# Gate/up units of an FFN: product order 1, 2, 5, 6, 7, 3, 4 instead of 1, 5, 6, 2, 7, 3, 4, gate half before up half, and a new order of VectorE's work

## The chip, the cores and the metric

The kernel runs on one NeuronCore of a Trainium2 chip. Its engines work side by side, each through its own queue in program order: TensorE (matmuls, PE in the profile, with the weight loads as PEld), VectorE (DVE), ScalarE (ACT), GpSimd (POOL) and SyncE (SP), which issues nearly all DMAs. They wait for each other by semaphores. The metric is the device time of one execution in microseconds (us); the time before is the median of three runs.

## The reference

A transformer block with adaptive layer norm: six modulation rows from a small product, a linear-attention block, and a gated FFN. All inputs are bfloat16; the sequence has S = 2048 rows, D = 1024, F = 3584.

```python
mod = (_silu(c) @ w_mod).reshape(c.shape[0], 6, 1, -1)      # sa, ca, ga, sb, cb, gb
h = _layernorm(x) * (1 + ca) + sa
x = x + ga * _A_ref(h, A_wqkv, A_wo)                        # linear attention, 32 heads
h = _layernorm(x) * (1 + cb) + sb
x = x + gb * _B_ref(h, B_w_gate, B_w_up, B_w_down)

def _B_ref(x, w_gate, w_up, w_down):
    return _gelu(x @ w_gate) * (x @ w_up) @ w_down
```

## The kernel before

The program is written as one list of operations with the memory ranges that they read and write; every operation waits for the earlier ones it depends on. Each engine runs its own operations in the order of the list. Only the attention part (up to the mark at L1679) is put into another order by a planner with costs and due times (`reorder`, L1862); the FFN stages, which the change touches, run exactly as written.

**Gate/up stage** (about 242 to 605 us of the span). It has 28 units: 2 halves of the sequence (1024 rows each) by 14 blocks of 256 columns of F. A unit computes gate and up for 256 columns and 1024 rows by a Winograd form of the 2x2 block product, with 7 products instead of 8, each for gate (t = 0) and up (t = 1). A product is 4 matmuls of 128x128 weights by 512 columns per t, so a unit has 56 matmuls (`prod`, L1464). Products 1 and 2 are plain bfloat16 ones. Products 5, 6, 7, 3, 4 are of sums and differences and run in float32r: `t_sum` (L1438, two 512-wide VectorE ops for each of the differences 0, 1, 2, 4; number 3 is a plain copy on ScalarE, L1427) makes the five weight operands `tp0` to `tp4` for products 5, 6, 7, 3, 4, and `s_sum` (L1418, 8 ops of 1024 wide per half of the sequence) makes the four state operands. `ar_copy` (L1404) is ScalarE's copy of the fifth.

PSUM's eight banks are four pairs, gate and up each: BA for products 1 and 2, BE for product 5, BB for products 6, 7 and 4, BC for product 3. What joins them:

- `pcp` (L1470, ScalarE) copies product 1 from BA to BB, and product 2 then adds onto BA, product 6 onto BB.
- `escp` (L1473, ScalarE) evicts product 5 to SBUF.
- `padd` (L1476, VectorE): after product 6, BC = BB + product 5; after product 7, BE = BB + product 5. Product 3 adds onto BC, product 4 onto BB.
- `gelu` (L1481, ScalarE) of the gate bank and `y_out` (L1485, VectorE), the product with the up bank, for four outputs: BA after product 2, BE after 7, BC after 3, BB after 4. The last output's `y_out` is held back and emitted in the next unit, behind the first half of its product 1; `y_store` then sends the unit's result to HBM.

A matmul that writes a bank, as the first of its product, waits until the bank has been read: product 2 for `pcp`, product 7 for `padd` after product 6, product 4 for `padd` after product 7, and `pcp(1)` itself waits for the held `y_out` that reads the up bank of BB. Product 6 needs both copies of `pcp`.

`unit(v)` (L1502) walks the products in `order`; behind each product it emits what belongs to it and then runs hooks, small pieces of other work spread over the units with `hook(v, k, fn)` (run behind product k of unit v). ScalarE's layer norm for the second half of the sequence lies in units 1 to 8 (sum behind product 6, square sum behind 7, normalisation behind 3, the last followed by a DMA transpose on SP); the modulation `mod2` in units 5 to 9; the second half's `s_sum` in units 10 to 13; from unit 14 on the weight sums of the down stage (`b_sum`, L1577, one 512-wide op per hook, four per block of the down weights) and their raw loads (`raw_load`, L1560 to 1567, SP). Unit 0 has its own order (ORD0: 1, 2, 5, 6, then 7, 3, 4 with the last attention chunks between) and is left alone by the change of the default order.

**Down stage** (from about 605 us): the same Winograd form with 8 row blocks; `dprod` (L1611), `dpcp` (L1644), `descp` (L1648), `dpadd` (L1652), `a_sum` (L1605) play the parts of `prod`, `pcp`, `escp`, `padd`, `s_sum`; `lws(n)` emits the next n of the remaining weight sums.

Of the kernel before, what the change touches and what calls it, by code (L numbers as in the profile page):

```python
# [346 lines left out]
def bass_adaLN_cond__linear_attn_block__geglu_ffn__prompt_kernel(  # L347
# [18 lines left out]
    with ExitStack() as es:  # L366
# [410 lines left out]
        def mod2(p, h, c0, n, dc0=0, dc1=NDC):  # L777
            mods(h2ap, r_h2p, (p, h), sc2, c0 * P, (c0 + n) * P, dc0, dc1, "h2")
# [320 lines left out]
        late = {}  # L1099
# [298 lines left out]
        ND2 = NDC // 2  # L1398
        S32 = [[t_.ap().bitcast(f32) for t_ in r_] for r_ in SS]
        T32 = [t_.ap().bitcast(f32) for t_ in TP]  # L1400

        def ar_copy(p):
            for k in (0, 2):
                sch.op(A, lambda e, k=k: e.activation(A22R[p][:, k:k + 2, :], H2[p][1][:, ND2 + k:ND2 + k + 2, :], ACTF.Copy),  # L1404
                       rd=r_h2(p, 1, ND2 + k, ND2 + k + 2), wr=r_ar(p, k, k + 2), note=f"arcp {p}.{k}")

# [38 lines left out]
        def prod(u, t, k, dcs=range(ND2)):  # L1445
            p = u // NFP
            if k in (1, 2):
                r = k - 1
                lhs = lambda dc: (WT[u % 2][:, t, r * ND2 + dc, 0:P], r_wt(u % 2, t, t + 1, r * ND2 + dc, r * ND2 + dc + 1))
                rhs = lambda dc: (H2[p][0][:, r * ND2 + dc, :], r_h2(p, 0, r * ND2 + dc, r * ND2 + dc + 1))  # L1450
            else:
                ti = {5: 0, 6: 1, 7: 2, 3: 3, 4: 4}[k]
                lhs = lambda dc: (TP[ti][:, t, dc, :], r_tp(ti, t, t + 1))
                if k == 4:
                    rhs = lambda dc: (A22R[p][:, dc, :], r_ar(p, dc, dc + 1))
                else:
                    si = {5: 0, 6: 1, 7: 2, 3: 3}[k]
                    rhs = lambda dc: (SS[p][si][:, dc, :], r_ss(p, si, dc, dc + 1))
            b = {1: BA, 2: BA, 5: BE, 6: BB, 7: BB, 4: BB, 3: BC}[k] + t
            fresh = k in (1, 5)  # L1460
            o = None
            for dc in dcs:
                (l_, rl), (r_, rr) = lhs(dc), rhs(dc)
                o = sch.op(T, lambda e, l_=l_, r_=r_, dc=dc: e.matmul(PS(b), l_, r_, start=fresh and dc == 0, stop=dc == ND2 - 1, skip_group_check=True),  # L1464
                           rd=rl + rr, pwr=(pr(b) if dc == 0 else ()), note=f"ffn u{u} P{k} {t} dc{dc}", overwrite_ok=True)
            if dcs[-1] == ND2 - 1:
                pset_writer(b, o)
# [31 lines left out]
        def hook(v, k, fn):  # L1499
            HK.setdefault((v, k), []).append(fn)  # L1500

        def unit(v, order=(1, 5, 6, 2, 7, 3, 4)):  # L1502
            more = v + 1 < 2 * NFP
            for k in order:
                if isinstance(k, tuple):
                    wo_chunk(*k)
                    continue
                if callable(k):
                    k()
                    continue  # L1510
                late = v == 0 and k == 2
                gb_, gk, yl, yh = (None, 1, 0, 0) if late else {2: (BA, 0, 0, 0), 7: (BE, 1, 1, 1), 3: (BC, 0, 1, 0), 4: (BB, 0, 0, 1)}.get(k, (None, 1, 0, 0))
                if k > 2:
                    for dc in range(ND2):
                        for t in range(2):
                            prod(v, t, k, [dc])
                for t in range(2):
                    if k < 3:
                        prod(v, t, k)
                    if k == 1:  # L1520
                        if held[0]:
                            held[0]()
# [12 lines left out]
                if k == 2 and v + 2 < 2 * NFP:  # L1535
                    wt_dma(v + 2)
                if k == 4:
                    held[0] = lambda: y_out(ig, BB, v, 0, 1)
                elif gb_ is not None:
                    y_out(ig, gb_, v, yl, yh)  # L1540
                if k == 1:
                    if v == 0:
                        ar_copy(0)
                    else:
                        t_sum(v, 4)
                if more:
                    if k == (3 if v == 0 else 5):
                        t_sum(v + 1, 0)
                    if k == (3 if v == 0 else 2):
                        t_sum(v + 1, 1)  # L1550
                    if k == 3:
                        t_sum(v + 1, 3)
                        t_sum(v + 1, 2)
                for f_ in HK.pop((v, k), ()):
                    f_()

# [156 lines left out]
        for i in range(4):  # L1713
            hook(i + 1, 2, lambda i=i: x1_store(i))
        for n in range(4):
            hook(5 + n // 2, (7, 4)[n % 2], lambda n=n: mod2(1, 0, 0, 4, 2 * n, 2 * n + 2))
        hook(9, 7, lambda: mod2(1, 1, 0, 4, 0, 3))
        hook(9, 4, lambda: mod2(1, 1, 0, 4, 3, 5))
        hook(9, 6, lambda: mod2_act(1, 1, 0, 4, 5, 6))
        hook(9, 3, lambda: mod2_act(1, 1, 0, 4, 6, 8))  # L1720
        hook(10, 3, lambda: ar_copy(1))
        for n in range(8):
            i, j = divmod(n, 2)
            hook(10 + n // 2, (7, 4)[n % 2], lambda i=i, j=j: s_sum(1, i, j))
        hook(12, 2, lambda: raw_load(0))
        hook(13, 2, lambda: raw_load(1))
        ew = b_sums(range(NEA + 2))
        for n in range(4 * NEA):
            v, k = 14 + n // 2, (7, 4)[n % 2]
            hook(v, k, lambda: next(ew)())  # L1730
            if n % 4 == 3 and 2 + n // 4 < NEA:
                hook(v, k, lambda n=n: raw_load(2 + n // 4))
# [3 lines left out]
        hook(24, 2, lambda: raw_load(6))  # L1736
        hook(26, 2, lambda: raw_load(7))
        hook(26, 7, lambda: next(ew)())
        hook(26, 4, lambda: next(ew)())
        V_ = 2 * NFP - 1  # L1740
        hook(V_, 5, lambda: a_sum(0, 0, NEA))
        hook(V_, 5, lambda: next(ew)())
        hook(V_, 6, lambda: (raw_load(8), a_sum(1, 0, NEA), a_sum(4, 0, NEA)))
        hook(V_, 2, lambda: (raw_load(9), raw_load(10), next(ew)(), next(ew)()))
        hook(V_, 7, lambda: (raw_load(11), raw_load(12)))
        hook(V_, 3, lambda: (next(ew)(), next(ew)()))
        hook(V_, 4, lambda: next(ew)())

        for v in range(2 * NFP):
# [20 lines left out]
        dprod(0, 5, 0, NEA)  # L1770
        descp(0)
        a_sum(2, 0, NEA)
        lws(3)
        dprod(0, 6, 0, NEA)
        dpadd(0, BC)
        a_sum(3, 0, NEA)
        dprod(0, 2, 0, NEA)
        for l in range(2):
            y_load(1, l, 0, NEA)
# [1 line left out]
        dpadd(0, BE)  # L1781
        dprod(0, 3, 0, NEA)
        dprod(0, 4, 0, NEA)
        lws(6)
        for k in range(NEA, NKP):
            for s_ in range(2):
                for c in range(2):
# [148 lines left out]
```

## Time and profile before

| | |
|---|---|
| median of the runs (lowest to highest) | 791.15 us (790.52 to 792.69) |
| profiled execution, its own time | 790.65 us |
| its span, first to last instruction | 788.8 us |
| TensorE busy | 775.3 us (98%) |
| VectorE, ScalarE, GpSimd busy | 636.1 (81%), 342.5 (43%), 43.9 us (6%) |
| granted TensorE clock | 1.000 |
| gate/up unit in steady state (units 14 to 26) | 12.60 us |

Busy times are sums over the span; matmuls are pipelined, so a row's length (0.38 to 0.39 us for a 512-wide matmul) is longer than the step from one matmul to the next. In a group of n like matmuls the step is the group's length less one row, over n - 1. A timeline line reads: start in us, length in us, engine, source line, operation, output <- inputs, shape, how many were merged, and in square brackets how long the engine sat idle before it and what ended that wait. A waits line reads: engine and line, what it waited for, the total in us, how often, the longest. In the chain of work each piece is a stretch in which the end of the program hung on the named engine.

### The profile page before, as it was taken

The numbers are of one execution on the slowest core, as the hardware profiler recorded it, in microseconds if no ns is written. First come the engines' busy times: TensorE is split into PE (matmuls) and PEld (weight loads), VectorE is DVE, ScalarE is ACT, GpSimd is POOL, SyncE is SP. The second block draws the span as 40 slices with busy tenths as digits, with TensorE's granted clock in tenths as the row PEclk, the third lists the DMA queues.
The fourth block names the chain that finished last, engine by engine and source line by source line (L and its number), as shares of the span: only waits on it lengthen the run. The fifth ranks groups of instructions, "written<-read, shape, count | busy, mean of one in ns | idle before, by whom it ended". The sixth has DMA issues, their size and how long they took to land. (4 is left out here: it accounts for less than half of the span.)

```text
span 788.8 us, 11024 instructions
## 1 busy us (share of the span) xinstructions
PE 775.3 (98%) x3840; PEld 495.6 (63%) x3904; DVE 636.1 (81%) x1078; ACT 342.5 (43%) x582; POOL 43.9 (6%) x126
## 2 busy tenths in 40 slices
PE   7999999999999999999999999999999999999998
PEld 4444445666445667777666767777776576666766
DVE  6799899983598877888999888898989786567664
ACT  2497743232583576675634444453545011111110
POOL 2131300000230001010000000000000000000000
PEclk9999999999999999999999999999999999999999
DMA  9789749836596378556355557555546354434340
GB/s 288 246 175 240 169 109 237 207 72 130 133 256 167 116 205 253 154 135 170 99 151 148 159 168 233 141 147 147 142 117 203 102 170 128 140 113 139 109 141 27
DMA packets 211407, 125.93 MB, mean 160 GB/s; under 512 B 70668, under 2 KB 201748, under 8 KB 211352
## 3 DMA queue, kind: packets, MB, share of 16 engines
q1 hardware_dynamic: 211336, 125.23, 58.5%
q8 instruction: 31, 0.51, 0.3%
q14 instruction: 24, 0.20, 0.1%
q10 hardware_dynamic: 16, 0.00, 0.0%
HBM read 88.35 MB, written 23.22 MB: 141 GB/s over the span
## 5 line engine op out<-in xcount | busy, mean ns | idle before, releaser
L1464 PE MATMUL ps_all<-ss,tp 128*128 128x512 f32 x896 | 226.2, 403 | 1.1 <-ACT ps_all L1470 0.6
L1464 PEld LDWEIGHTS ps_all<-ss,tp 128*128 128x128 f32 x896 | 167.7, 188 | 43.6 <-ACT ps_all L1470 2.2
L1481 ACT ACTIVATE ge<-ps_all 128x512 f32<-128x512 f32 x112 | 66.7, 596 | 134.7 <-DVE ps_all L1476 83.2
L1611 PE MATMUL ps_all<-bt,xs 128*128 128x512 f32 (+1 forms) x485 | 118.5, 399 | 0.9 <-DVE ps_all L1652 0.9
L1611 PEld LDWEIGHTS ps_all<-bt,xs 128*128 128x128 f32 x485 | 91.1, 188 | 22.3 <-DVE ps_all L1652 1.4
L1485 DVE TENSOR_TENSOR yr<-ge,ps_all 128x512 bf16<-128x512 f32 x112 | 76.7, 685 | 31.6 <-PE ps_all L1464 17.8
L1476 DVE TENSOR_TENSOR ps_all<-ps_all,es 128x512 f32<-128x512 f32 x112 | 72.4, 691 | 8.7 <-PE ps_all L1464 7.5
L1438 DVE TENSOR_TENSOR tp<-wt 128x512 fp32r<-128x512 bf16 x112 | 72.1, 684 | 1.3
L1438 DVE TENSOR_TENSOR tp<-wt,tp 128x512 fp32r<-128x512 bf16 x112 | 72.0, 683 | 0.0
L1611 PE MATMUL ps_all<-bx,yl 128*128 128x512 bf16 (+2 forms) x269 | 59.8, 360 | 0.7
L965 PE MATMUL ps_all<-h1T,wq 128*128 128x512 bf16 x256 | 56.7, 379 | 0.0
L914 PE MATMUL ps_all<-wk,h1T 128*128 128x512 bf16 x239 | 55.3, 379 | 1.1 <-DMA wk<-in_A_wqkv_dram 0.5
L1299 PE MATMUL ps_all<-w,pq 128*128 128x512 bf16 x251 | 55.9, 379 | 0.4
L1644 ACT ACTIVATE ps_all<-ps_all 128x512 f32<-128x512 f32 x8 | 4.7, 582 | 117.4 <-PE ps_all L1611 117.4
L1464 PE MATMUL ps_all<-ar,tp 128*128 128x512 f32 x224 | 55.3, 389 | 0.0
L903 ACT ACTIVATE eb<-ps_all 128x512 f32<-128x512 f32 x64 | 36.4, 593 | 37.1 <-PE ps_all L914 15.4
L1464 PE MATMUL ps_all<-h21a,wt 128*128 128x512 bf16 x210 | 50.1, 380 | 1.0
L1464 PE MATMUL ps_all<-h20a,wt 128*128 128x512 bf16 x210 | 50.0, 380 | 0.9
L1464 PEld LDWEIGHTS ps_all<-ar,tp 128*128 128x128 f32 x224 | 42.1, 188 | 8.7
L1470 ACT ACTIVATE ps_all<-ps_all 128x512 f32<-128x512 f32 x56 | 32.6, 582 | 30.6 <-DVE yr L1485 15.4
L965 PEld LDWEIGHTS ps_all<-h1T,wq 128*128 128x128 bf16 x256 | 25.0, 98 | 30.0
L1299 PEld LDWEIGHTS ps_all<-w,pq 128*128 128x128 bf16 x256 | 24.7, 98 | 30.3 <-issue 0.5
(146 smaller groups left out, 903.8 us busy)
## 6 DMA issues: line engine op xcount, KB each, us to landing
wt<-in_B_w_gate_dram SPq DMA_DIRECT2D x28, 512.0 KB, 4.0
wt<-in_B_w_up_dram SPq DMA_DIRECT2D x28, 512.0 KB, 5.2
scr_y<-yr SPq DMA_DIRECT2D x56, 256.0 KB, 2.9
yl<-scr_y SPq DMA_DIRECT2D x12, 832.0 KB, 4.3
wmst<-in_w_mod_dram SPq DMA_DIRECT2D x6, 1024.0 KB, 5.7
wmq<-in_w_mod_dram SPq DMA_DIRECT2D x8, 512.0 KB, 6.1
rb<-scr_rd SPq DMA_DIRECT2D x32, 128.0 KB, 2.9
scr_x<-xall SPq DMA_DIRECT2D x4, 1024.0 KB, 7.1
```

The source lines that it names most:

```text
L903: sch.op(A, lambda e: e.activation(EB[i][:, :], PS(bank), ACTF.Exp), prd=pr(bank), wr=rng, note=f"{note}.exp")
L914: o = sch.op(T, lambda e, dc=dc: e.matmul(PS(bank), H1[sg][:, ci, dc, :], W_[:, dc, jg * 512:(jg + 1) * 512], start=(dc == 0), stop=(dc == ...
L965: o = sch.op(T, lambda e, dc=dc: e.matmul(PS(b), WQ[:, dc, qc * P:(qc + 1) * P], H1[sg][:, :, dc, :], start=(dc == 0), stop=(dc == NDC - 1 ...
L1299: last[half] = sch.op(T, lambda e, g=g, half=half: e.matmul(PS(b0 + half), PQ[sg][:, g, ci * P:(ci + 1) * P], W2[:, g, half * 512:(half + ...
L1438: sch.op(V, lambda e, t=t: e.tensor_tensor(TP[k][:, t, :, :], in0[:, t, :, :], in1[:, t, :, :], ALU.subtract), rd=r0[t:t + 1] + (r1[t:t + ...
L1464: o = sch.op(T, lambda e, l_=l_, r_=r_, dc=dc: e.matmul(PS(b), l_, r_, start=fresh and dc == 0, stop=dc == ND2 - 1, skip_group_check=True) ...
L1470: sch.op(A, lambda e: e.activation(PS(BB + t), PS(BA + t), ACTF.Copy), prd=pr(BA + t), pwr=pr(BB + t), note="pcp")
L1476: sch.op(V, lambda e: e.tensor_tensor(PS(dst + t), PS(BB + t), ES[t][:, :], ALU.add), prd=pr(BB + t), rd=r_2k(OFF_ES[t], f"es{t}"), pwr=pr ...
L1481: sch.op(A, lambda e: e.activation(GE[i][:, :], PS(b), ACTF.Gelu_apprx_tanh), prd=pr(b), wr=r_2k(OFF_GE[i], f"ge{i}"), note="gelu")
L1485: sch.op(V, lambda e: e.tensor_tensor(YR[:, 2 * (v % 2) + l, h * SGW:(h + 1) * SGW], GE[i][:, :], PS(b + 1), ALU.mult), rd=r_2k(OFF_GE[i], ...
L1611: pend_ = sch.op(T, lambda e, l_=l_, r_=r_, i=i: e.matmul(PS(b, c0, c1), l_, r_, start=fresh and i == 0, stop=i == n - 1, skip_group_check ...
L1644: sch.op(A, lambda e: e.activation(PS(BB + t), PS(BA + t), ACTF.Copy), prd=pr(BA + t), pwr=pr(BB + t), note="pcp")
```

## The change

- **Order of products** of units 1 to 27: 1, 2, 5, 6, 7, 3, 4 instead of 1, 5, 6, 2, 7, 3, 4.
- **Gate before up.** Products 5, 6, 7, 3, 4 ran matmul by matmul alternately for gate and up; now all four gate matmuls come first, as products 1 and 2 already had it. The GELU of product 7's output is emitted behind the gate half.
- **VectorE's weight differences.** Difference 0 for the next unit moves from behind product 5 to behind product 7. Differences 1 and 2 move from the unit before (behind products 2 and 3) into the unit that uses them: behind product 1, after the held last output of the unit before, and ahead of difference 4.
- **Hooks.** Those behind product 4 move to behind product 2 of the next unit (modulation, state sums, weight sums with their raw loads). `ar_copy(1)` is split over units 10 and 11, behind product 6. In unit 27 the raw loads and weight sums are spread over products 2, 6, 7, 3 and 4 in another way.
- **Down stage.** Of the nine weight sums that `lws` emits ahead of the plain products, three stood ahead of the first `dpadd`; now one follows behind `a_sum(3)`, and eight behind product 4.

```diff
-        def unit(v, order=(1, 5, 6, 2, 7, 3, 4)):
+        def unit(v, order=(1, 2, 5, 6, 7, 3, 4)):
...
-                gb_, gk, yl, yh = (None, 1, 0, 0) if late else {2: (BA, 0, 0, 0), 7: (BE, 1, 1, 1), 3: (BC, 0, 1, 0), 4: (BB, 0, 0, 1)}.get(k, (None, 1, 0, 0))
-                if k > 2:
-                    for dc in range(ND2):
-                        for t in range(2):
-                            prod(v, t, k, [dc])
+                gb_, gk, yl, yh = (None, 1, 0, 0) if late else {2: (BA, 0, 0, 0), 7: (BE, 0, 1, 1), 3: (BC, 0, 1, 0), 4: (BB, 0, 0, 1)}.get(k, (None, 1, 0, 0))
                 for t in range(2):
-                    if k < 3:
-                        prod(v, t, k)
+                    prod(v, t, k)
...
                     else:
+                        t_sum(v, 1)
+                        t_sum(v, 2)
                         t_sum(v, 4)
                 if more:
-                    if k == (3 if v == 0 else 5):
+                    if k == (3 if v == 0 else 7):
                         t_sum(v + 1, 0)
-                    if k == (3 if v == 0 else 2):
-                        t_sum(v + 1, 1)
                     if k == 3:
                         t_sum(v + 1, 3)
-                        t_sum(v + 1, 2)
...
         for n in range(4):
-            hook(5 + n // 2, (7, 4)[n % 2], lambda n=n: mod2(1, 0, 0, 4, 2 * n, 2 * n + 2))
+            hook(5 + (n + 1) // 2, (7, 2)[n % 2], lambda n=n: mod2(1, 0, 0, 4, 2 * n, 2 * n + 2))
         hook(9, 7, lambda: mod2(1, 1, 0, 4, 0, 3))
-        hook(9, 4, lambda: mod2(1, 1, 0, 4, 3, 5))
+        hook(10, 2, lambda: mod2(1, 1, 0, 4, 3, 5))
...
-        hook(10, 3, lambda: ar_copy(1))
+        hook(10, 6, lambda: ar_copy(1, (0,)))
+        hook(11, 6, lambda: ar_copy(1, (2,)))
         for n in range(8):
             i, j = divmod(n, 2)
-            hook(10 + n // 2, (7, 4)[n % 2], lambda i=i, j=j: s_sum(1, i, j))
+            hook(10 + (n + 1) // 2, (7, 2)[n % 2], lambda i=i, j=j: s_sum(1, i, j))
...
         for n in range(4 * NEA):
-            v, k = 14 + n // 2, (7, 4)[n % 2]
+            v, k = 14 + (n + 1) // 2, (7, 2)[n % 2]
...
         hook(26, 7, lambda: next(ew)())
-        hook(26, 4, lambda: next(ew)())
         V_ = 2 * NFP - 1
+        hook(V_, 2, lambda: (raw_load(9), raw_load(10), next(ew)()))
         hook(V_, 5, lambda: a_sum(0, 0, NEA))
-        hook(V_, 5, lambda: next(ew)())
         hook(V_, 6, lambda: (raw_load(8), a_sum(1, 0, NEA), a_sum(4, 0, NEA)))
-        hook(V_, 2, lambda: (raw_load(9), raw_load(10), next(ew)(), next(ew)()))
-        hook(V_, 7, lambda: (raw_load(11), raw_load(12)))
-        hook(V_, 3, lambda: (next(ew)(), next(ew)()))
+        hook(V_, 7, lambda: (raw_load(11), raw_load(12), next(ew)(), next(ew)()))
+        hook(V_, 3, lambda: (next(ew)(), next(ew)(), next(ew)()))
         hook(V_, 4, lambda: next(ew)())
...
         a_sum(2, 0, NEA)
-        lws(3)
         dprod(0, 6, 0, NEA)
         dpadd(0, BC)
         a_sum(3, 0, NEA)
+        lws(1)
         dprod(0, 2, 0, NEA)
...
         dprod(0, 4, 0, NEA)
-        lws(6)
+        lws(8)
```

More of the change, by code (lines that the diff above doesn't have):

```diff
@@ L1400, in bass_adaLN_cond__linear_attn_block__geglu_ffn__prompt_kernel, with ar_copy @@
         T32 = [t_.ap().bitcast(f32) for t_ in TP]
-        def ar_copy(p):
-            for k in (0, 2):
+        def ar_copy(p, ks=(0, 2)):
+            for k in ks:
                 sch.op(A, lambda e, k=k: e.activation(A22R[p][:, k:k + 2, :], H2[p][1][:, ND2 + k:ND2 + k + 2, :], ACTF.Copy),
```

## The prediction

> **What bounds the kernel now.** I read the page's busy shares first, then the chain of work in order of time, then the timelines of single units.
>
> ```profile
> PE 775.3 (98%) x3840; PEld 495.6 (63%) x3904; DVE 636.1 (81%) x1078; ACT 342.5 (43%) x582; POOL 43.9 (6%) x126
> 472.03 12.53 PE ps_all L1464 x55
> 484.56 0.07 issue
> 484.63 12.53 PE ps_all L1464 x55
> ```
>
> TensorE bounds the kernel, and in units 14 to 26 of the gate/up stage a unit takes 12.60 us with no stall. So only two things can move the time: a cheaper stream of matmuls, or new and removed waits of TensorE. Cadences, from the timelines: eight float32r matmuls span 1.98 us and eight bfloat16 ones 1.90 us; less the last one's own 0.389 and 0.380 us, and over seven steps, that is 0.227 and 0.217 us.
>
> ```profile
> 489.80 1.98 PE L1464 MATMUL ps_all<-ar,tp 128*128 128x512 f32 x8
> 491.61 1.90 PE L1464 MATMUL ps_all<-h21a,wt 128*128 128x512 bf16 x8
> ```
>
> How a wait reaches TensorE is seen in three places: the add of product 6 in a steady unit, a stalled unit (a ScalarE copy releases a weight load) and the start of the down stage (a VectorE add releases one).
>
> ```profile
> 496.10 1.07 PE L1464 MATMUL ps_all<-ss,tp 128*128 128x512 f32 x4
> 497.05 0.70 DVE L1476 TENSOR_TENSOR ps_all<-ps_all,es 128x512 f32<-128x512 f32 x1 [0.52 <-PE ps_all L1464]
> ...
> 392.55 0.58 ACT L1470 ACTIVATE ps_all<-ps_all 128x512 f32<-128x512 f32 x1 [0.56 <-DVE yr L1485]
> 393.18 0.30 PEld L1464 LDWEIGHTS ps_all<-ss,tp 128*128 128x128 f32 x2 [0.56 <-ACT ps_all L1470]
> ...
> 610.72 0.69 DVE L1652 TENSOR_TENSOR ps_all<-ps_all,es 128x512 f32<-128x512 f32 x1
> 611.46 0.50 PE L1611 MATMUL ps_all<-bt,xs 128*128 128x512 f32 x1 [0.90 <-DVE ps_all L1652]
> ```
>
> Before the add the four matmul starts are 496.10, .33, .55 and .78; the gate half's last one is the third (products alternate gate and up), so the add starts 0.50 us after that start. It lasts 0.70. From an add's or copy's end to the load it releases is 0.05 us (393.13 to 393.18, 611.41 to 611.46). The first float32r matmul then runs 0.50 instead of 0.39: 0.11 us of it is the load.
>
> The last view is ScalarE in units 2 to 9, which follow units with layer-norm work on it:
>
> ```profile
> 298.05 0.60 ACT L1481 ACTIVATE ge<-ps_all 128x512 f32<-128x512 f32 x1 [2.90 <-DVE ps_all L1476]
> 298.55 1.14 ACT L701 ACTIVATE xl<-xall,mv 128x1024 bf16<-128x1024 bf16 x1
> ...
> 301.19 1.24 ACT L689 ACTIVATE xl<-xall,nm,rs 128x1024 bf16<-128x1024 bf16 x1
> 302.33 0.59 ACT L1481 ACTIVATE ge<-ps_all 128x512 f32<-128x512 f32 x1
> 303.01 0.58 ACT L1470 ACTIVATE ps_all<-ps_all 128x512 f32<-128x512 f32 x1
> ```
>
> From product 7's GELU (298.05) to the next unit's first copy of product 1 (303.01) ScalarE has no gap: 4.96 us.
>
> **The change part by part.** Let s be the start of a unit's product 1, u that of its product 6; both per unit.
>
> *A. Fewer changes of type.* 16 x 0.216 + 40 x 0.227 us (0.2267 unrounded) is 12.52; the 0.08 left of 12.60 belongs to two changes bfloat16 to float32r and back. The new order has one: -0.04 us in 27 units (unit 0 already ran 1, 2, 5, 6), **-1.1**. That gate and up no longer alternate banks costs nothing: the down products stay in one bank and have the same 0.227.
>
> *B. Product 7 right behind 6.* Product 7 overwrites the banks that the add of product 6 reads, so its first weight load waits for that add. Before, product 2 lay between (8 x 0.216 = 1.73 us) and hid it. Now the gate half ends after four matmuls: add 0.50 us after the fourth start, 0.70 long, 0.05 to the load, 0.11 to the matmul, 1.36 us in all; TensorE would be ready after the remaining five steps, 5 x 0.227 = 1.13. Stall 0.23. The up half's add starts after its own fourth matmul, so it is late by nothing more (about 0.01). After stalls the float32r stream runs at 0.231 to 0.236 for a few matmuls, about 0.03. Together 0.265 x 27 = **+7.2**. Ends: 0.12 if the load could come early, 0.33 if the second add also stalls: 3.2 to 8.9. I take 0.265, since every term is a row of this trace.
>
> One row against one rule: the load at 393.18 was not issued until the copy had ended. The Trainium skill (TensorE: Matmul & The Clock Gate, "Step-by-step: what each phase is for") says that the queue pulls weight loads ahead of running matmuls. If that held for a load whose semaphore is still open, the 0.11 would vanish, 27 x 0.11 = 3.0 us, and the sum would be 3.0 lower. The trace speaks for the row.
>
> *C. Product 2 right behind 1.* Product 2 accumulates where ScalarE's copy reads product 1. Unit 0 already does this: its copy at 243.43 ended at 244.01, the load came at 244.06, and its 15 bfloat16 matmuls ran on without a gap. A steady unit's copy starts 1.07 us after s (492.69 against 491.61) and ends at 1.66, load at 1.71; product 2 is due at 1.74: no stall, 0.03 us of cover. In units 2 to 9 ScalarE is the last. Product 7 now starts at u + 2.08, its gate add at u + 3.26 and ends at 3.96, the GELU starts at u + 4.00, and 4.96 later, u + 8.96, the copy. The unit ends at u + 7.52 (four products of 1.81 and 0.265), so the copy starts at s + 1.44, ends at 2.02, the matmul starts at 2.09 instead of 1.74: 0.35 us. Eight times 0.35 = 2.8; unit 10, behind two modulation ops on ScalarE, about 0.2, and two units with modulation on VectorE about 0.1 each: **+3.2**. Bounds: 0 if ScalarE's chain shrinks, 5.3 if each is 0.6.
>
> *D. VectorE's queue.* The six weight differences of a unit come behind the previous unit's last output instead of partly ahead. The old price of lateness: a unit of 13.03 us four times (units 10 to 13, where VectorE also has two 1.14 us sums) and 0.8 us in unit 1 (product 1 starts at 262.01 and 275.45, 13.44 us, where its neighbours take 12.64). Unit 1: only two differences, not six, precede the output, which then starts near s + 0.7: **-0.8**. Units 10 to 13 lose their 4 x 0.43 = 1.7, as product 6 comes at s + 5.3 instead of s + 3.6. But by VectorE's pitch (0.605 per 512-wide op) the last output starts at s + 0.93 behind a 1.14 us sum; then that output, six differences and the next output, 8 x 0.605, and another sum: 0.93 + 4.84 + 1.14 = 6.91, where the add of product 6 could start at 5.31 + 0.68 + 0.50 = 6.49. That is 0.42 late in units 11 to 14, +1.7: **0 net**, ends -1.7 and +1.5. In units with weight sums of 0.605 the add's turn comes at 0.42 + 4.84 + 0.61 = 5.87, before 6.49: hidden, with 0.6 us to spare.
>
> *E. End of the stage.* Three weight sums stood ahead of the first add of the down stage; TensorE lost 1.278 - 0.216 = 1.06 there (610.18 to 611.46). One now comes after it. In unit 27 a 0.9 us activation sum precedes product 6's add, about +0.25: **-0.8**. Ends -1.1 and 0. The later 0.6 us sums move between places where plain products run.
>
> *Queues.* SP's weight loads for the unit after next wait for product 2 and for the unit's weight differences, so they go out near s + 5 instead of s + 6.6 (307.25 against a unit start of 300.69); they land 4.0 and 5.2 us later (the page's DMA issues) and are first read at the end of the next unit, some 15 us on. Raw loads on SP move by up to half a unit, and their first readers come two units later; those of the last unit are read in the down stage. POOL does nothing new. The float32r copy of the second half's states, 2 x 1.04 us on ScalarE, is split over two units, behind product 5's evictions, where ScalarE now idles until u + 4.00. All of it costs nothing under this cover; if it were gone, the two copies would delay product 2 like the layer-norm work, by some 0.4 us each.
>
> Sum: -1.1 + 7.2 + 3.2 - 0.8 + 0 - 0.8 = **+7.7 us**. The profiled execution took 790.65 us for a span of 788.8, 0.5 below the median of the runs, 791.15; so 798.35 by the one and 798.85 by the other. I forecast 798.5.
>
> **The rivals.** *Not slower:* product 7's stall is hidden, because the add ends before TensorE gets there. It decides at 0.23 us: the way from the fourth matmul's start to product 7 would have to be 1.13 instead of 1.36. Price: without B, 791.15 + 0.5 = 791.7. For it: the old order alternated halves, so no row shows this very pair; against it: each step is measured. *Faster:* neither B nor C appears, 791.15 - 2.7 = 788.4; that needs ScalarE's 4.96 us chain to hide too. *Half:* B at its low end and C absent, 791.15 + 0.5 = 791.7 as well (7.7 - 4.0 - 3.2). *VectorE becomes the bound:* it is busy 11.2 us of a 12.6 us unit; if the outputs' order lets it fall behind by 0.4 us in the 13 units with weight sums too, 13 x 0.42 = 5.5 more, 804. Against it stands the 0.6 us of slack. *The clock falls:* if small stalls in each unit cost TensorE its clock for one product, 27 x 1.81 = 49 us more, 847; the stalled units at 391 to 417 us kept a granted clock of 1.00. The Trainium skill (same page, "A second HAM failure mode: psum-queue depth-cycling") describes such micro-idles between groups; the trace disagrees so far.
>
> **How the numbers follow.** Forecast 0.68, its own range 795 to 802. VectorE bound 0.14, no stall or half of it 0.11, faster 0.06, clock 0.01. This kernel can't tell less than 0.3%, 2.4 us, from no change. Faster 0.06, same 0.11, slower 0.83. The range 793.5 to 804.0 leaves out the faster cases, the hidden stall and what lies above 804, some 0.2.
>
> **What would show it.** Right: in each steady unit a gap of about 0.23 us ahead of product 7, its load released by the add at L1476, units of about 12.82 us; in units 2 to 9 a second gap of 0.35 us ahead of product 2, released by ScalarE's copy, units near 13.2; no 1.06 us gap at the start of the down stage; units 11 to 14 still near 13.2. Wrong: steady units of 12.56 us, the load of product 7 issued before the add's end, or VectorE without idle time ahead of product 6's add.

## The result, and the profile after

The changed kernel takes 800.97 us (median of 4 runs, 800.80 to 801.37); the kernel before took 791.07 us beside it (4 runs, 790.52 to 792.69). The ratio is 1.0122, with a 95% interval of 1.0105 to 1.0140: slower by 9.9 us. The profiled execution took 800.83 us for a span of 799.0, against 790.65 and 788.8, so 10.2 us have to be found.

The busy shares on the page of the kernel after:

```profile
PE 786.4 (98%) x3904; PEld 492.1 (62%) x3904; DVE 638.6 (80%) x1078; ACT 348.2 (44%) x582; POOL 48.8 (6%) x126
```

No engine has more instructions that count. TensorE's sum is 11.1 us higher, but a matmul that waits for its operands is a longer row, and 64 matmul records are missing from the trace of before (3840 against 3904), so this sum proves little. Two things on it are worth a look: TensorE is still at 98%, and POOL has 4.9 us more with the same 126 instructions. That second number is the clue to the part of the loss that the prediction had not seen.

The waits of TensorE's weight loads (engine and line, what it waited for, total us, how often, longest) in the kernel after:

```profile
PEld ps_all L1464 <- ACT ps_all L1470: 21.6, 56, 1.0
PEld ps_all L1464 <- DVE ps_all L1476: 11.9, 28, 0.7
```

Before, the first of these lines read 2.8 us in 6 waits, and there was no second one. 56 is two halves of product 1 in each of 28 units: product 2 now waits for ScalarE's copy. 28 is one a unit in the 27 units, and one more: product 7 waits for VectorE's add of product 6. A wait of the weight load is longer than TensorE's own loss, because loads run ahead of the matmuls (in a steady unit the load ahead of product 2 idles for 0.3 us, and the matmuls go on without a gap); the loss itself is read from the lengths of units.

The length of a unit is taken from one start of product 1 to the next (in three of the runs below the record of product 1's first matmul is missing from unit 2 on; the unit is then counted from 0.23 us ahead of the second):

| us | before | after |
|---|---|---|
| unit 1 | 13.44 | 12.81 |
| units 2 to 9, mean | 12.63 | 13.55 |
| unit 10 | 12.60 | 12.88 |
| units 11 to 14, each | 13.03 | 13.17 |
| units 15 to 26, each | 12.60 | 12.81 to 12.87 |
| unit 27 | 12.60 | 12.95 |
| units 1 to 27 together | 343.00 | 353.78 |
| down stage to the end | 183.8 | 182.7 |

The 27 units lose 10.78 us, the rest after them gains 1.17, and unit 1 starts 0.59 later. That last difference arises in the first 25 us of the span, where both kernels wait for the modulation weights with the same code; no part of the change is there. The table also puts a reading of before right: the four units of 13.03 us are 11 to 14, one later than the prediction has them, and the steady 12.60 us holds from unit 15 on, not 14. No sum of the prediction hangs on that.

**Product 7, in a steady unit.** Timeline of the kernel after:

```profile
545.12 2.68 PE L1464 MATMUL ps_all<-ss,tp 128*128 128x512 f32 x10
...
545.62 0.70 DVE L1476 TENSOR_TENSOR ps_all<-ps_all,es 128x512 f32<-128x512 f32 x1 [0.64 <-PE ps_all L1464]
546.37 1.23 PEld L1464 LDWEIGHTS ps_all<-ss,tp 128*128 128x128 f32 x6 [0.38 <-DVE ps_all L1476]
546.53 0.70 DVE L1476 TENSOR_TENSOR ps_all<-ps_all,es 128x512 f32<-128x512 f32 x1 [0.21 <-PE ps_all L1464]
```

The gate half's add ends at 546.32 and the weight load goes out at 546.37, 0.05 us later, as at the two places shown of before. The two matmul starts around the load are 0.345 and 0.335 apart instead of 0.227: a stall of 0.23 us. The add itself had waited 0.64 us for TensorE, so VectorE was not late here.

**Product 2, in units 2 to 9.** Timeline of the kernel after, where the unit begins at 316.06:

```profile
312.41 0.60 ACT L1481 ACTIVATE ge<-ps_all 128x512 f32<-128x512 f32 x1 [2.07 <-DVE ps_all L1476]
...
314.00 1.29 DVE L1438 TENSOR_TENSOR tp<-wt 128x512 fp32r<-128x512 bf16 x2
...
314.30 0.44 POOL L703 TENSOR_SCALAR ve<-st 128x1 f32<-128x1 f32 x1 [3.58 <-ACT xl L701]
314.52 1.15 ACT L1427 ACTIVATE tp<-wt 128x512 fp32r<-128x512 bf16 x2
314.82 0.90 POOL L704 TENSOR_TENSOR rs<-ve,neghalf 128x1 f32<-128x1 f32 x1
...
315.79 0.19 POOL L706 TENSOR_TENSOR nm<-mv,rs 128x1 f32<-128x1 f32 x1
316.02 1.24 ACT L689 ACTIVATE xl<-xall,nm,rs 128x1024 bf16<-128x1024 bf16 x1 [0.35 <-POOL nm L706]
...
317.17 0.58 ACT L1481 ACTIVATE ge<-ps_all 128x512 f32<-128x512 f32 x1
...
317.83 1.30 ACT L1470 ACTIVATE ps_all<-ps_all 128x512 f32<-128x512 f32 x2
...
318.47 0.39 PE L1464 MATMUL ps_all<-h20a,wt 128*128 128x512 bf16 x1 [0.51 <-ACT ps_all L1470]
```

ScalarE's copy starts 1.77 us after the unit does, not 1.44. And ScalarE's chain from product 7's GELU (312.41) to the copy (317.83), which had no gap before and took 4.96 us, now takes 5.42 us and has one gap: ahead of the normalisation at L689 ScalarE sat idle for 0.35 us, waiting for POOL. The gap costs 0.46 and not 0.35, because ScalarE otherwise starts the normalisation 0.11 us before the end of the operation ahead of it (before: L1427 from 300.16 for 1.14, L689 from 301.19). POOL's three small operations are the same as ever, but two of them are longer. The same three in the kernel before (timeline):

```profile
299.93 0.19 POOL L703 TENSOR_SCALAR ve<-st 128x1 f32<-128x1 f32 x1 [5.81 <-ACT xl L701]
...
300.20 0.57 POOL L704 TENSOR_TENSOR rs<-ve,neghalf 128x1 f32<-128x1 f32 x1
300.30 0.69 DVE L1485 TENSOR_TENSOR yr<-ge,ps_all 128x512 bf16<-128x512 f32 x1 [0.90 <-ACT ge L1481]
...
300.85 0.19 POOL L706 TENSOR_TENSOR nm<-mv,rs 128x1 f32<-128x1 f32 x1
```

From the first start to the last end they took 1.11 us there and take 1.68 now. What differs beside them is VectorE: weight difference 0 (L1438, both inputs in SBUF) now stands behind product 7, and runs from 314.00 to 315.29. Before, VectorE was idle or at an output (L1485, one input in PSUM). That POOL is slowed by it is a guess at this point; three of the kernels below bear on it.

**Clock.** Each line of this view gives a stretch, its length, the busy time of TensorE, its weight loads, VectorE, ScalarE and POOL, the granted clock, the DMA share and GB/s. The first is a unit among 2 to 9, the second a steady one, both of the kernel after:

```profile
317.00:330.60 13.60, 13.09 (x58) 8.81 (x57) 10.82 (x18) 9.03 (x16) 1.74 (x4) 1.00 0.52 136
542.40:555.20 12.80, 12.80 (x57) 8.73 (x56) 11.25 (x19) 6.26 (x12) 0.00 (x0) 1.00 0.57 163
```

The granted clock stayed at 1.00 although every unit now has a stall or two. It was 1.00 as the mean over each of the four runs as well.

### The profile page after: what moved, and what is told of

Same layout as the page of the kernel before. It is cut to its first block, busy times and chain, and to the rows that moved or that the text cites. A ratio compares the mean times of both kernels' runs of the same rounds, so it can differ in the third digit from the quotient of the medians.

```text
span 799.0 us, 11039 instructions
## 1 busy us (share of the span) xinstructions
PE 786.4 (98%) x3904; PEld 492.1 (62%) x3904; DVE 638.6 (80%) x1078; ACT 348.2 (44%) x582; POOL 48.8 (6%) x126
## 4 chain that ended last, share of the span: by engine, by line
PE 84%; DVE 6%; DMA 3%; SPq 2%; ACT 2%; issue 2%; POOL 1%; POOLq 0%; ACTq 0%; DVEq 0%
PE ps_all L1464 36%; PE ps_all L1605 22%; PE ps_all L1299 7%; PE ps_all L965 7%; PE ps_all L929 6%; PE ps_all L914 5%; DVE tp L1438 2%; DMA mtb<-mb 1%; DVE yr L1485 1%; SPq L627 1%; DMA wmq<-in_w_mod_dram 1%; DVE ps_all L1476 1%; DVE ss L1418 1%; ACT xl L701 1%; DMA wst<-in_B_w_down_dram 1%
## 5 line engine op out<-in xcount | busy, mean ns | idle before, releaser
L1464 PE MATMUL ps_all<-ss,tp 128*128 128x512 f32 x896 | 222.1, 401 | 1.3 <-DVE ps_all L1476 1.2
L1464 PEld LDWEIGHTS ps_all<-ss,tp 128*128 128x128 f32 x896 | 165.1, 188 | 49.9 <-DVE ps_all L1476 11.9
L1476 DVE TENSOR_TENSOR ps_all<-ps_all,es 128x512 f32<-128x512 f32 x112 | 77.6, 698 | 34.0 <-PE ps_all L1464 33.9
L1485 DVE TENSOR_TENSOR yr<-ge,ps_all 128x512 bf16<-128x512 f32 x112 | 75.0, 681 | 16.7 <-ACT ge L1481 7.2
L1438 DVE TENSOR_TENSOR tp<-wt 128x512 fp32r<-128x512 bf16 x112 | 71.9, 683 | 0.0
L1438 DVE TENSOR_TENSOR tp<-wt,tp 128x512 fp32r<-128x512 bf16 x112 | 71.9, 682 | 0.0
L1605 PE MATMUL ps_all<-bx,yl 128*128 128x512 bf16 (+1 forms) x282 | 61.2, 361 | 0.0
L914 PE MATMUL ps_all<-wk,h1T 128*128 128x512 bf16 x248 | 56.9, 379 | 0.5 <-DVE h1T L754 0.2
L1464 PE MATMUL ps_all<-h20a,wt 128*128 128x512 bf16 x224 | 52.2, 380 | 4.2 <-ACT ps_all L1470 4.2
L1473 ACT ACTIVATE es<-ps_all 128x512 f32<-128x512 f32 x56 | 33.6, 600 | 38.1 <-PE ps_all L1464 38.1
```

Source lines behind the costliest of these rows:

```text
L914: o = sch.op(T, lambda e, dc=dc: e.matmul(PS(bank), H1[sg][:, ci, dc, :], W_[:, dc, jg * 512:(jg + 1) * 512], start=(dc == 0), stop=(dc == ...
L1438: sch.op(V, lambda e, t=t: e.tensor_tensor(TP[k][:, t, :, :], in0[:, t, :, :], in1[:, t, :, :], ALU.subtract), rd=r0[t:t + 1] + (r1[t:t + ...
L1473: sch.op(A, lambda e: e.activation(ES[t][:, :], PS(BE + t), ACTF.Copy), prd=pr(BE + t), wr=r_2k(OFF_ES[t], f"es{t}"), note="escp")
L1476: sch.op(V, lambda e: e.tensor_tensor(PS(dst + t), PS(BB + t), ES[t][:, :], ALU.add), prd=pr(BB + t), rd=r_2k(OFF_ES[t], f"es{t}"), pwr=pr ...
L1485: sch.op(V, lambda e: e.tensor_tensor(YR[:, 2 * (v % 2) + l, h * SGW:(h + 1) * SGW], GE[i][:, :], PS(b + 1), ALU.mult), rd=r_2k(OFF_GE[i], ...
L1605: pend_ = sch.op(T, lambda e, l_=l_, r_=r_, i=i: e.matmul(PS(b, c0, c1), l_, r_, start=fresh and i == 0, stop=i == n - 1, skip_group_check ...
```

## The experiments

The theory at this point: the loss is the order of products, through two waits that share no cause, B (product 7 behind the add of product 6) and C (product 2 behind ScalarE's copy), and C is larger than forecast because the moved difference 0 slows POOL. The rivals: the loss comes from the new order on VectorE; C is ScalarE's chain alone; and the two waits are one problem, so that either cure helps with both. All kernels are edits of the kernel after, but for the one on the down stage, which is the kernel before with one edit.

### The old order of products with everything else new

```diff
-        def unit(v, order=(1, 2, 5, 6, 7, 3, 4)):
+        def unit(v, order=(1, 5, 6, 2, 7, 3, 4)):
```

> The changed kernel with the old order of products, 1, 5, 6, 2, 7, 3, 4, in units 1 to 27; all else of the change is kept. My theory (two new waits of TensorE made by the order: product 7 behind the add of product 6, product 2 behind ScalarE's copy): both vanish and the second change of type comes back, so steady units go from 12.84 to 12.60 us, units 2 to 9 from 13.54 to 12.62, units 11 to 14 from 13.17 to 12.6; the gate/up stage from 353.8 to about 340.5 us, the time to about 787.7 us, below the kernel before. Rival (VectorE's new queue is what costs, the order matters little): steady units stay above 12.8 us and the time near 798.

Measured: 787.47 us (4 runs, 787.13 to 789.02) beside 791.10 for the kernel before, ratio 0.9958 (0.9941 to 0.9974). Units take 12.60 us but for three, the longest 12.73, and all together 340.41, against 353.78 of the kernel after. So the order of products costs 13.4 us, and the rest of the change is a gain of 3.4 us in span against before: 2.6 in the units (0.84 in unit 1, four times 0.43 in units 11 to 14), 1.2 in the down stage, less 0.4 of a later start. VectorE's new order is not the cause of the loss; with the old order of products it lengthens no unit by more than 0.13 us. POOL is slow here too (L704 has a median of 894 ns in units 1 to 8) and ScalarE waits 0.29 to 0.35 us for it in each of them, but the first product that needs ScalarE's copies, product 6, comes eight matmuls later in this order, and the wait costs TensorE next to nothing.

### Without the moved difference

```diff
-                    if k == (3 if v == 0 else 7):
+                    if k == (3 if v == 0 else 7) and not 1 <= v <= 8:
                         t_sum(v + 1, 0)
```

> The changed kernel without weight difference 0 of units 2 to 9 (16 VectorE operations left out; product 5 of those units reads old weights). In these units GpSimd's three small operations for the layer norm take 0.44, 0.90 and 0.19 us instead of 0.19, 0.57 and 0.19 before, and ScalarE waits 0.35 us for them. Theory: they are slow because VectorE now runs difference 0 at the same moment; without it they take 0.19, 0.57, 0.19 again, ScalarE's wait goes, units 2 to 9 fall from 13.54 to 13.20 us and the time by 2.7 to about 798.3. Rival (they are slow for another reason, or the rest of ScalarE's chain holds the copy back anyway): rows as in the changed kernel, units of 13.5 us, 801.

Measured: 797.30 us (4 runs, 796.75 to 798.89), ratio 1.0079 (1.0064 to 1.0094). VectorE leaves out the 16 operations of difference 0 for units 2 to 9. Units 2 to 9 fall from 13.55 to 13.10 us, and the other units stay within 0.05. The eight POOL operations of L704 in this stage (source and engine, then shortest, median and longest in ns, first and last start), first in the kernel after, then in this one:

```profile
L704 POOL TENSOR_TENSOR rs<-ve,neghalf x8: 891/894/898, 274.2 to 369.0; 128x1 f32<-128x1 f32 x8
```

```profile
L704 POOL TENSOR_TENSOR rs<-ve,neghalf x8: 565/568/587, 273.6 to 365.3; 128x1 f32<-128x1 f32 x8
```

And the timeline of this kernel, where ScalarE's normalisation shows no idle time ahead of it any more:

```profile
312.63 0.19 POOL L703 TENSOR_SCALAR ve<-st 128x1 f32<-128x1 f32 x1 [3.58 <-ACT xl L701]
312.86 1.15 ACT L1427 ACTIVATE tp<-wt 128x512 fp32r<-128x512 bf16 x2
...
313.55 0.19 POOL L706 TENSOR_TENSOR nm<-mv,rs 128x1 f32<-128x1 f32 x1
313.89 1.24 ACT L689 ACTIVATE xl<-xall,nm,rs 128x1024 bf16<-128x1024 bf16 x1
```

With difference 0 gone, POOL is back at its old durations, ScalarE no longer waits for it, and 0.45 us of each unit's loss go with it (0.34 had been expected, the idle time without the 0.11 us of overlap that is lost with it). The other 0.27 us (13.10 less 12.835, the mean of the steady units) is ScalarE's chain without POOL's share. What this run alone cannot tell is whether the two operations harm POOL by running at the same time or by some other way that taking them out removes. The kernel with the old order can, since two of its eight units have POOL's operations at another place against difference 0. Timeline of one of them:

```profile
348.80 1.29 DVE L1438 TENSOR_TENSOR tp<-wt 128x512 fp32r<-128x512 bf16 x2
...
349.43 0.72 POOL L703 TENSOR_SCALAR ve<-st 128x1 f32<-128x1 f32 x1 [5.49 <-ACT xl L701]
...
350.01 0.68 DVE L1485 TENSOR_TENSOR yr<-ge,ps_all 128x512 bf16<-128x512 f32 x1
350.23 0.56 POOL L704 TENSOR_TENSOR rs<-ve,neghalf 128x1 f32<-128x1 f32 x1
```

Here nearly the whole of L703 lies beside the second half of difference 0, which ends at 350.09, and L703 takes 0.72 us; L704 starts behind it and has its old 0.56 us. In the other unit they take 0.71 and 0.62, in the six remaining ones 0.43 to 0.45 and 0.89 to 0.90, as in the kernel after. So the operation that runs beside the difference is the one that is slow.

The Trainium skill ("SBUF — State Buffer", section "Who interferes with whom") says that a VectorE instruction with two SBUF inputs contends with a GpSimd instruction that reads SBUF, since its second input comes through a read interface that the two engines share, and that one with at most one SBUF input, outside the modes in which VectorE uses two ports, does not. The runs agree: 0.89 us beside L1438 (two inputs in SBUF), 0.57 us beside L1485 (one in PSUM). The interface itself no trace shows.

### The normalisation behind the next unit's product 1

```diff
-            hook(v, 3, lambda c_=c_: ln2_rows(c_))
+            hook(v + 1, 1, lambda c_=c_: ln2_rows(c_))
```

> The changed kernel with one piece moved: ScalarE's normalisation (1.24 us) of units 1 to 8, with its transpose on SP, goes from behind product 3 to behind product 1 of the next unit, so it stands behind the two bank copies in ScalarE's queue instead of ahead of them. Theory: the stall ahead of product 2 is wholly ScalarE's chain (0.27 us of it the chain, 0.44 the slower GpSimd ahead of the normalisation), so it vanishes though GpSimd stays slow: units 2 to 9 from 13.54 to 12.84 us, the time by 5.6 to about 795.4. Rival (part of the stall has another source, such as the last output on VectorE or the weights): units 2 to 9 stay above 13.0 us, the time near 798 or above.

Measured: 795.76 us (4 runs, 795.24 to 796.63), ratio 1.0060 (1.0044 to 1.0075). Units 2 to 9 take 12.83 us each, the same as the steady units, and the 27 units together 348.05: 5.73 us less than in the kernel after. POOL is as slow as there:

```profile
L704 POOL TENSOR_TENSOR rs<-ve,neghalf x8: 891/892/895, 275.1 to 364.9; 128x1 f32<-128x1 f32 x8
```

The timeline shows why this no longer matters. A unit starts at 289.13, and the GELU and both copies now come ahead of the normalisation:

```profile
288.64 0.59 ACT L1481 ACTIVATE ge<-ps_all 128x512 f32<-128x512 f32 x1
290.20 0.58 ACT L1470 ACTIVATE ps_all<-ps_all 128x512 f32<-128x512 f32 x1 [0.97 <-PE ps_all L1464]
...
291.06 0.58 ACT L1470 ACTIVATE ps_all<-ps_all 128x512 f32<-128x512 f32 x1 [0.28 <-PE ps_all L1464]
...
291.56 1.23 ACT L689 ACTIVATE xl<-xall,nm,rs 128x1024 bf16<-128x1024 bf16 x1
```

The copy starts 1.07 us after the unit, as in a steady unit of the kernel before, and waits for TensorE instead of the other way round. So the whole of C, 5.7 us with the 0.03 that each of these units had lost before, hung on where ScalarE's normalisation stands in its queue, and B stayed exactly where it was: the two waits are independent, and the rival by which one cure helps with both falls.

### Gate and up alternating in the new order

```diff
+                if k > 2:
+                    for dc in range(ND2):
+                        for t in range(2):
+                            prod(v, t, k, [dc])
                 for t in range(2):
-                    prod(v, t, k)
+                    if k < 3:
+                        prod(v, t, k)
```

> The changed kernel with gate and up matmuls alternating again in products 5, 6, 7, 3, 4 (the new order of products kept). Theory: the stall ahead of product 7 is the way from the gate half's last matmul (0.50 to the add, 0.70 the add, 0.05, 0.11 the load, 1.36 in all) less the steps that TensorE still has; these are now two instead of five, so the gate stall is 1.36 - 0.45 = 0.91, and the second add, 0.605 behind the first, adds 0.605 - 0.227 = 0.38: 1.29 instead of 0.23 per unit, units of 13.9 us, 28.6 us more in all, about 829.6. Rival (a fixed cost of handing over between engines, the same however the halves lie): units of 12.85 us, 801.

Measured: 834.91 us, one run. Steady units take 13.85 to 13.88 us: 1.0 us more than with gate before up, as worked out from when each half ends. When the halves alternate, gate's last matmul is the seventh instead of the fourth, so both adds are late. Timeline of this kernel:

```profile
362.20 1.30 DVE L1476 TENSOR_TENSOR ps_all<-ps_all,es 128x512 f32<-128x512 f32 x2 [0.59 <-PE ps_all L1464]
...
362.96 0.19 PEld L1464 LDWEIGHTS ps_all<-ss,tp 128*128 128x128 f32 x1 [1.06 <-DVE ps_all L1476]
362.96 1.79 PE L1464 MATMUL ps_all<-ss,tp 128*128 128x512 f32 x5 [0.64 <-DVE ps_all L1476]
```

The two adds overlap a little, 1.30 us for two of 0.70 (the first ends at 362.90); the load again goes out 0.06 us behind it. So gate before up is what keeps B small in the new order, and B's arithmetic holds at a second distance. The miss is units 2 to 9, which take 15.19 to 15.27 us, and unit 10 with 14.60; for that reason the time came out 5.3 us above the expectation. They are 1.36 us longer than the steady ones, where the kernel after had 0.72: the stall ahead of product 2 grew as well, to a step of 1.5 to 1.6 us, though the unit had become longer. That is ScalarE's chain again, summed too low again; how much of it is the later GELU was not taken apart.

### Half products in between

```diff
+        HALF = ((1, 0), (1, 1), (2, 0), (2, 1), (5, 0), (6, 0), (5, 1), (6, 1), (7, 0), (3, 0), (7, 1), (3, 1), (4, 0), (4, 1))
...
-        def unit(v, order=(1, 2, 5, 6, 7, 3, 4)):
+        def unit(v, order=HALF):
...
+                    if more and v > 0 and k == 7 and t == 0:
+                        t_sum(v + 1, 0)
...
-            hook(10 + (n + 1) // 2, (7, 2)[n % 2], lambda i=i, j=j: s_sum(1, i, j))
+            hook(10 + (n + 1) // 2, (7, 6)[n % 2], lambda i=i, j=j: s_sum(1, i, j))
...
-            v, k = 14 + (n + 1) // 2, (7, 2)[n % 2]
+            v, k = 14 + (n + 1) // 2, (7, 6)[n % 2]
```

Here the gate half of product 6 is followed by the up halves of 5 and 6 before product 7's gate half comes, and difference 0 is built behind product 7's gate half.

> The changed kernel with the float32r products in half products, gate g and up p: 1g 1p 2g 2p 5g 6g 5p 6p 7g 3g 7p 3p 4g 4p; difference 0 goes behind 7g, and VectorE's state and weight sums of product 2 go behind product 6. Now nine steps (2.04 us) instead of five lie between the fourth matmul of a half of product 6 and the same half of product 7, more than the 1.36 us that the add needs. Theory: the stall ahead of product 7 vanishes, steady units of 12.56 us; in units 2 to 9 the stall ahead of product 2 stays, 0.35 us if GpSimd is fast again (12.91), so about 342 us for the stage and 789 for the whole. Rival (product 7 waits for something else, or another wait takes its place): units above 12.8 us, 799 or more.

Measured: 794.49 us (4 runs, 794.07 to 794.87), ratio 1.0040 (1.0025 to 1.0055); 789 was expected. In units 1 and 15 to 27 it did all that was expected: 12.56 us each. That is 0.04 us below the 12.60 of the old order, which is part A of the prediction by itself, and B is gone with eight matmuls between the add's input and product 7. The miss is in the rest: units 2 to 9 take 13.17 to 13.21 us (units 6 and 7: 13.6), units 10 to 13 take 12.73 to 12.89, unit 14 takes 13.66. POOL is fast here, median 568 ns, and the timeline shows an output of VectorE beside it, not a difference:

```profile
312.78 1.29 DVE L1485 TENSOR_TENSOR yr<-ge,ps_all 128x512 bf16<-128x512 f32 x2
...
313.28 0.19 POOL L703 TENSOR_SCALAR ve<-st 128x1 f32<-128x1 f32 x1 [2.90 <-ACT xl L701]
313.55 0.57 POOL L704 TENSOR_TENSOR rs<-ve,neghalf 128x1 f32<-128x1 f32 x1
...
314.43 1.24 ACT L689 ACTIVATE xl<-xall,nm,rs 128x1024 bf16<-128x1024 bf16 x1 [0.26 <-POOL nm L706]
```

So VectorE at work beside POOL isn't enough to slow it: with an output running over nearly all of the same operation (to 314.07) it takes 0.57 us. Ahead of units 6 and 7 it takes 0.66 and 0.70, beside two modulation operations of VectorE (L754, one wide input, in SBUF). ScalarE waits for POOL all the same, 0.26 us (0.35 and 0.39 ahead of units 6 and 7), since in this order no GELU lies between the square sum and the normalisation, and its own work ends earlier. The matmul starts of these units show where they lose the time: the one step ahead of product 2's first matmul is 0.83 us instead of 0.22 (302.85 to 303.69), 0.93 in units 6 and 7. So it is C once more, with a fast POOL; the mixed order below bears that out. Units 6 and 7 have a second stall, of 0.23 us, ahead of product 7's gate half: VectorE's add of product 6 comes late there, at 334.93 behind two operations of L754, and the load goes out 0.05 us behind it, at 335.68. That is B again, through a busy VectorE. Unit 10 has the same. In units 11 to 13 a weight load of product 4 waits for the add of product 7 (0.29 us at 405.71). Units 12 and 13 also lose 0.13 us ahead of the up half of product 2, and why stays open. Unit 14 loses its time elsewhere: a weight load at 441.97 waits 1.05 us for the state sum at L1418, which the moved hook had put behind two adds of that unit. By this row it is that hook, and not the order, that has to be put back there; no run puts it back alone.

### Only the sums of the down stage

The kernel before, with the weight sums of the down stage placed as the change places them:

```diff
         a_sum(2, 0, NEA)
-        lws(3)
         dprod(0, 6, 0, NEA)
         dpadd(0, BC)
         a_sum(3, 0, NEA)
+        lws(1)
...
         dprod(0, 4, 0, NEA)
-        lws(6)
+        lws(8)
```

> The kernel before with one part of the change: of the nine weight sums at the start of the down stage none stands ahead of its first add, one behind the second activation sum and eight behind product 4. Theory: the 1.06 us that TensorE lost ahead of product 7 of that stage (610.18 to 611.46 us) vanishes and nothing takes its place: from the first matmul of the down stage to the end 182.7 us instead of 183.8, gate/up units as before. Rival (the sums are missed later, by the plain products or the next row block): 183.8 or more.

Measured: 789.76 us, one run. The down stage and what follows take 182.7 us against 183.8, and the units are as before. VectorE in this kernel (timeline), where the first add had been late by 1.06 us of TensorE's time before:

```profile
608.20 0.96 DVE L1605 TENSOR_TENSOR xs<-yl 128x768 fp32r<-128x768 bf16 x1 [0.95 <-PE ps_all L1611]
609.64 0.70 DVE L1652 TENSOR_TENSOR ps_all<-ps_all,es 128x512 f32<-128x512 f32 x1 [0.49 <-PE ps_all L1611]
```

The add now waits 0.49 us for TensorE, and not behind weight sums. All of part E's gain in the down stage is this edit alone.

### A mixed order

Half products, the normalisation moved, and the old order of whole products in units 10 to 14; the state sums stay behind product 2, the weight sums go behind product 6. The lines of the edit that matter:

```diff
+        HALF = ((1, 0), (1, 1), (2, 0), (2, 1), (5, 0), (6, 0), (5, 1), (6, 1), (7, 0), (3, 0), (7, 1), (3, 1), (4, 0), (4, 1))
...
-            hook(v, 3, lambda c_=c_: ln2_rows(c_))
+            hook(v + 1, 1, lambda c_=c_: ln2_rows(c_))
...
-            unit(v, *([ORD0] if v == 0 else []))
+            unit(v, *([ORD0] if v == 0 else [(1, 5, 6, 2, 7, 3, 4)] if 10 <= v <= 14 else []))
```

> What the runs point to put together: the changed kernel with half products (as in the run with them: 1g 1p 2g 2p 5g 6g 5p 6p 7g 3g 7p 3p 4g 4p, difference 0 behind 7g), the normalisation behind the next unit's product 1, and the old order of whole products in units 10 to 14, where VectorE has the most to do. Theory: neither stall is left and one change of type is saved in 22 of 27 units: units of 12.56 us, in units 10 to 14 12.60, the stage about 339.5 us, the time about 786.6 us, 0.1% below the run with the old order (787.5), too little to tell from it; about 0.6% below the kernel before. Rival (halves bring a wait of their own where ScalarE is loaded): units 2 to 9 above 12.8 us, the time above 788.5.

Measured: 786.94 us (5 runs, 786.32 to 788.31), ratio 0.9949 (0.9936 to 0.9961). Units with half products take 12.56 us without exception, units 2 to 9 among them, so with the normalisation moved nothing is left of the 0.6 us that they lost above. Units 10 to 13 take 12.60, unit 14 takes 12.63; together 339.35. This is below both kernels. It can't be told from the old order with the rest of the change, 787.47 us: the units are 1.06 us shorter, which is 0.13% of the time.

## Why the prediction was right, and where it was off

The direction, the two mechanisms and the places were right, and the time lay in the range. Of the 10.2 us in span, 7.7 were forecast. That the time still fell in the range is owed to the range's width: the largest miss, C, lies above the upper bound of 5.3 that the prediction itself gave it, and comes from a wait that it had not seen. Point by point, worked out from the table of units:

| part | forecast | measured | from |
|---|---|---|---|
| A and B, fewer type changes and product 7 behind 6 | -1.1 + 7.2 = 6.1 | 6.3 | 27 x (12.835 - 12.60) |
| C, product 2 behind 1 | 3.2 | 5.5 | 8 x (13.55 - 12.835), unit 10's 0.06, less the 0.25 that units 2 to 9 already lost |
| D, VectorE's queue | -0.8 + 0 | -0.8 - 0.4 | unit 1's 0.84; 4 x 0.335 - 4 x 0.43 |
| E, end of the stage and down stage | -0.8 | -1.05 | -1.17 in the down stage, +0.12 in unit 27 |
| start of unit 1 | none | 0.6 | first 25 us, the same code |

*A* was shown by itself: 12.56 us a unit where nothing stalls in the new order (half products), against 12.60.

*B* was right in each of its terms. The stall is 0.23 us, the load leaves 0.05 us after the add, the matmuls around it are 0.11 late each, and steady units came out at 12.81 to 12.87 for 12.82. The chance that the stall would be hidden is out. So is the higher end, a second stall at the up half: its add waited for TensorE. The rule on weight loads that was weighed here would have taken 3.0 us off the sum; the load with a closed semaphore was not pulled ahead in this kernel either, at 546.37 as in the row that the prediction went by. Within units 15 to 26 the length creeps up from 12.81 to 12.87 us; none of the runs says why.

*C* is the term that was mis-sized: 3.2 us against 5.5. The prediction took ScalarE's chain from GELU to copy, 4.96 us, from the trace of before and moved it as a rigid piece, and it wrote off difference 0's move among VectorE's differences without asking who reads beside it. Instead the chain grew to 5.42 us by a wait for POOL, since POOL's L703 and L704 take 0.44 and 0.90 us instead of 0.19 and 0.57. ScalarE's chain as it stood gives 0.27 us a unit (0.35 forecast), POOL's slowness 0.45. Without difference 0 the one remains, and with the normalisation moved both are gone. That difference 0 slows POOL by running beside it is shown: L704 takes 0.89 us in the kernel after, where only the normalisation moved, and in six of eight units of the old order, 0.57 in the kernel before, where difference 0 was left out, and where an output ran beside, and in the old order's other two units the slowness goes over to L703 with the overlap. By what way the one slows the other, no run shows.

*D* was right for unit 1. For units 11 to 14 the mechanism was right, a VectorE that comes late to product 6's add behind a state sum, but the lateness is 0.335 us instead of 0.42, so that the net is a gain of 0.4. The chain of work in the kernel after shows it (start, length, what the end hung on):

```profile
415.61 0.64 DVE ss L1418
416.25 0.41 issue
416.67 0.70 DVE ps_all L1476
417.41 2.12 PE ps_all L1464 x8
```

State sum, add, and only then TensorE: here VectorE is what bounds. From 443.74 us on the same chain names TensorE alone, in 725 matmuls over 166.30 us, up to the add of unit 27 (the 0.23 us ahead of product 7 in each unit are too short for it to list), and the slack forecast at 0.6 us is the 0.64 us that the add waits in the steady unit above. So the rival by which VectorE becomes the bound everywhere is out. With the old order of products these four units take 12.60 to 12.62 us: D's part could have been a gain of 1.7.

*E* was right, with unit 27 at 0.12 us instead of 0.25, and its gain is the down stage's edit alone.

The clock's rival is out with 1.00 in both windows. The faster case would have needed both waits hidden; the mixed order shows what that is worth, 4.4 us below the kernel before, about the 2.7 that the rival named and the 1.7 of units 11 to 14 beside it.

## What to carry to other kernels

An operation moved on one engine has to be asked not only whom it waits for and who waits for it, but also what else will run beside it: here a move that cost its own engine nothing lengthened three tiny operations of another, which stood in a third engine's chain. When an accumulation is followed at once by one that needs its banks, count from the half that ends first to the load of the next, and put half a product of something else between: with eight matmuls in between the wait was gone, with four it was 0.23 us, one matmul. And look at where a rare long operation stands in the queue of the engine that now releases TensorE: moving one hook was worth more than half of the loss.

## What the runs showed of the hardware

GpSimd operations on 128x1 took 0.44 and 0.89 us instead of 0.19 and 0.57 while VectorE ran a 512-wide difference of two SBUF tiles, and their old durations while it ran a 512-wide product with an input in PSUM, or nothing. Where almost all of the shorter operation lay beside the difference, it took 0.72 us. That an operation of one element a partition could lose 0.3 us to this was not expected. And TensorE kept a granted clock of 1.00 through 27 units with a stall of 0.2 to 0.7 us in each, and as its mean also in the kernel with alternating halves, where a unit lost 1.3 us or more to stalls.
